# An adaLN block with a spectral filter and a SwiGLU on one core: load order, step order at the stage borders, and who does the x1 sums and the gate folds

## The chip, the core and the metric

The kernel runs on one core of one Trainium2 chip. Times are device microseconds of one execution; lower is better. The engines are named as in the profile: PE (TensorE matmul, PEld its weight loads), DVE (VectorE), ACT (ScalarE), POOL (GpSimd) and SP (SyncE, which here issues nearly all DMAs). "L302" is line 302 of the kernel before.

## The reference

Shapes: x is 2048 x 640 (S x D), all inputs bf16, F = 1728. Cut to what matters:

```python
mod = (silu(c) @ w_mod).reshape(1, 6, 1, 640)
sa, ca, ga, sb, cb, gb = mod[:, 0], mod[:, 1], mod[:, 2], mod[:, 3], mod[:, 4], mod[:, 5]
h = layernorm(x) * (1 + ca) + sa
X = rfft2(h) * (w_r + 1j * w_i)
x = x + ga * irfft2(X)
h = layernorm(x) * (1 + cb) + sb
x = x + gb * ((silu(h @ w_gate) * (h @ w_up)) @ w_down)
```

The Fourier transforms run over both axes (2048 and 640) and are computed as matmuls with tables.

## The kernel before

The 2048 rows lie on 128 partitions as 16 tiles t (row = 16 p + t). The order of all work is written out by hand: each engine runs its instructions in the order in which the program issues them, and the framework adds the semaphores. SP's queue runs its DMA issues in program order too, so an issue that waits holds all later ones.

**Phase 1, forward transform, tile by tile.** Steps with one or two letters are listed in a string `plan` (L391) and called one after the other. For tile t: `T` transposes x on PE (L258), `h` copies the result to `hT_all` (L261, ACT), `G` forms sums on PE (L266), `d` the statistics on DVE (L272, L274), `m` a small copy of the mean (L277, ACT), `p` and `r` root and reciprocal for a pair of tiles (L281 on ACT, L285 on DVE), `s` scales the row table by the tile's 1/sigma into `Gs` (L290, L291; POOL, for tiles 0 and 15 DVE), `B` the transform along D on PE (L296, PSUM `zps`, one buffer), `Z` takes the mean out (L302, DVE), `S` the first part of the transform along S on PE (L310, L311), `A` copies the result to `A_sb` (L321, ACT). `ca`, `ms`, `mh` and others compute the modulation vectors that phase 1 needs. `keep_warm` (L240) issues idle matmuls at the start.

**Loads.** SP issues x and the table G in groups of four tiles, then four DMAs (L196) that write the filter's rows in reversed order, 128 bytes a row, to a scratch tensor `Wneg` in DRAM, with two small ones each for the wrapped row; then `wm_sa`, `Ktab`, the filter itself (`Wb`, L205), the reversed filter (`Wq`, L207) and `KIt`.

**Phase 2, units of four columns.** 17 units u (unit 16 holds a single column). `t2` (L436) transposes a unit on PE, `transposed` (L432) two units by DMA. Then a software pipeline over `it`: `product(it)` multiplies by the filter on DVE (L487), `stage_x(it + 1)` computes the next unit's `xps` on PE and copies it to `X` on ACT (L466), where POOL adds a small term (L469); `stage_y(it - 1)` computes `yps` on PE and copies it to `Y2` (L509, ACT or DVE); `stage_e(it - 2)` computes `eps_` on PE and copies it to `Ep` (L539, ACT). All PSUM tiles of this phase rotate through four slots. `negate` (L412) prepares negated copies of the filter, for the first 33 columns on POOL (L416), and `mirror` (L548) those of `Ep` on DVE. Between iterations stand three groups of modulation matmuls: 50 at `it == 8` for the gate ga and for cb, the gate's transpose at `it == 9` (L229; its row goes to DRAM and comes back spread over the partitions by `gate_spread`, L238), 25 at `it == 10` for sb.

**Phase 3, inverse transform, tile by tile.** `s1inv` (L680) makes ten matmuls and a copy `VT` on ACT (L688); `dinv` (L692) five matmuls, then adds x to give x1: on DVE (L706), or, for the six tiles in `X1_ACT`, by five more matmuls (L702) and a copy on ACT (L704). The second layernorm's statistics of tiles 0 to 3 (`ln2_stats`, L626), their normalization (`ln2_xn`, L649, DVE), a DMA transpose (`ln2_turn`) and the affine step (`ln2_affine`, L660, DVE for even and ACT for odd blocks) are placed among the tiles.

**Feed-forward.** Four chunks sc of 512 rows. For each: `gu13` (L745), then 13 blocks fc of ten matmuls into `gu` (L757, two PSUM buffers), Silu on ACT (L760) and the product on DVE (L761). Into these blocks the next chunk's layernorm is placed: statistics at fc 1 to 4, `ln2_newton` (L632, twelve small DVE steps) at fc 5, `xn` at 6 and 7. In the first chunk the gate gb is folded into the rows of `Wd_sb` by DVE (L770), at the blocks that `folds` (L739) names. Then come the down matmuls (L795) and those of the last half block of 64 rows (`down13`, L790), and the sum with x1 and the store (L806, L809). For the last chunk's last half tile the accumulator is a fourth buffer of tag "o" (L786).

Of the kernel before, what the change touches and what calls it, by code (L numbers as in the profile page):

```python
# [104 lines left out]
def adaln_block_kernel(  # L105
# [83 lines left out]
    for g in range(1, 4):  # L189
        nc.sync.dma_start(x_sb[:, 4 * g:4 * g + 4, :], x_v[:, 4 * g:4 * g + 4, :])  # L190
        nc.sync.dma_start(Gtab[:, 4 * g:4 * g + 4], G_dram[:, 4 * g:4 * g + 4])
    for i, w_ in enumerate((A_w_i, A_w_r)):
        wv = w_.rearrange("(k2 k1) l -> k2 k1 l", k1=P)[:, :, 64:320]
        to = Wneg[i].rearrange("k1 k2 m l -> k2 k1 m l")
        for m in range(2):
            nc.sync.dma_start(to[:, 1:128, m], wv[:, 127:0:-1, 128 * m:128 * m + 64])  # L196
        w0 = wv[:, 0].rearrange("k2 (m l) -> k2 m l", m=2)[:, :, 0:64]
        nc.sync.dma_start(to[0:15, 0], w0[1:16])
        nc.sync.dma_start(to[15:16, 0], w0[0:1])
# [4 lines left out]
    for pl, w_ in ((0, A_w_i), (1, A_w_r)):  # L204
        nc.sync.dma_start(Wb[:, pl, :, 0:321], w_.rearrange("(k2 k1) l -> k1 k2 l", k1=P))  # L205
    for i in range(2):
# [37 lines left out]


    A_sb = big.tile([P, NL, NT, 2, NR], BF16, name="A_sb", tag="a")
    A_fl = A_sb[:].rearrange("p l t c r -> p (l t c r)")
    with tc.tile_pool(name="ph1", bufs=3) as ph1, \
# [64 lines left out]
        def acopy(t):  # L313
            ap = apss.pop(t)
            o = A_sb[:, :, t, :, :]
            i = ap[:, :, 0:325].rearrange("p c (r l) -> p l c r", r=NR)
            if t == NT - 1:
                nc.scalar.copy(o[:, 0:33], i[:, 0:33])
                nc.vector.tensor_copy(o[:, 33:NL], i[:, 33:NL])
            else:  # L320
                (nc.vector.tensor_copy if t in A_DVE else nc.scalar.copy)(o, i)  # L321
# [27 lines left out]
        def rv_out(_):  # L349
            nc.scalar.activation(rv, rvs[0][:].rearrange("p b q -> p (b q)")[:, 0:D], ACT.Copy, scale=0.2)  # L350
# [4 lines left out]
        keep_warm(ps1, "t1", 32)  # L355
# [28 lines left out]
        def sa_out(_):  # L384
# [4 lines left out]
        HT_DVE, A_DVE, S_DVE = (), (), (0, 15)  # L389
        GROUP = {0: 1, 1: 2, 3: 2, 5: 2, 7: 2, 9: 2, 11: 2, 13: 2, 15: 1}  # L390
        plan = (  # L391
# [6 lines left out]
        )  # L398
        steps = {"ca": mod_ca, "oc": one_ca, "rsD": rs_dve, "rsA": rs_act, "rvp": rv_mm, "rv": rv_out, "T": turn, "h": turned, "G": sums,
                 "d": stats, "m": mean, "p": root, "r": recip, "s": gscale, "B": dfwd, "Z": zcopy, "S": s1, "A": acopy,  # L400
                 "ms": mod_sa, "sacs": sa_cs, "mh": mod_sahat, "sh": sa_out}
        for w in plan.split():
            n = w.rstrip("0123456789")
            steps[n](int(w[len(n):] or 0))

# [5 lines left out]

    def negate(lo, hi, eng):  # L412
        eng(Wbr[:, 96:144, lo:hi], Wbr[:, 0:48, lo:hi])

    def neg_pool(o, i):
        nc.gpsimd.tensor_scalar(o, i, neg1[:], None, ALU.mult)  # L416

    def neg_dve(o, i):
        nc.vector.tensor_scalar(o, i, neg1[:], None, ALU.mult)

    with tc.tile_pool(name="ph2", bufs=2) as ph2, \
# [14 lines left out]
        def t2(u):  # L436
# [6 lines left out]
            (nc.vector.tensor_copy if u in (1, 3) else nc.scalar.copy)(o, ps[:, 0:n])  # L443
# [3 lines left out]
        def stage_x(u):  # L447
# [17 lines left out]
            X = ph2.tile([P, NI, 4], BF16, name="X", bufs=3)  # L465
# [49 lines left out]
        def stage_e(u):  # L515
# [26 lines left out]
            if u == 0:  # L542
                put(63, 0, 1)
                put(0, 1, 3)
            else:
                put(4 * u - 1, 0, 4)

        def mirror(lo, hi, eng):  # L548
            eng(Ep[:, :, 130 + lo:130 + hi, :], Ep[:, :, lo:hi, :])

        Y_ACT, E_DVE = (1, 3, 5, 7, 9, 11, 13, 15), ()

        negate(0, 17, neg_pool)
        negate(17, 33, neg_pool)
# [6 lines left out]
        t2(2)  # L561
        t2(3)
        for j, i in enumerate((2, 4)):
            nc.sync.dma_start(wm_g[:, :, D * j:D * (j + 1)], wm_v[:, :, D * i:D * (i + 1)])
        for it in range(NU + 2):
            if it < NU:
                product(it)
            if it + 1 < NU:
                stage_x(it + 1)
            if 0 <= it - 1 < NU:  # L570
                stage_y(it - 1)
            if it == 8:
# [303 lines left out]
```

## Time and profile before

| what | us |
|---|---|
| median of 3 runs (lowest, highest) | 284.56 (284.25, 288.49) |
| the profiled execution | 284.64 |
| its span, first to last instruction | 282.8 |
| PE busy, DVE, ACT, POOL | 263.9, 156.6, 113.9, 29.2 |
| mean granted PE clock | 0.994 of full |

The profile's page gives busy time by engine and by group of instructions, and the chain of work that ended last; the trace behind it can be asked for a timeline, for waits, and for a table of any stretches of time. A line of a timeline has the start, the duration, the engine, the line, the operation, what it writes and reads, how often, and in brackets how long the engine was idle before it and what released it. Several instructions in a row with one form are merged. Matmuls overlap, so a matmul's own duration (220 ns for 128 columns) is longer than the step from one to the next (56 ns).

### The profile page before, as it was taken

How to read it: one execution, taken by the hardware profiler on the slowest of the kernel's cores; microseconds unless marked ns; L12 is line 12 of the kernel's file. 1: busy time of each engine (PE TensorE's matmuls, PEld its weight loads, DVE VectorE, ACT ScalarE, POOL GpSimd, SP SyncE). 2: the span in 40 equal slices, each digit the busy share in tenths (PEclk: the TensorE clock that was granted, in tenths of full speed). 3: DMA queues.
4: the chain of work that ended last, by engine and by line, in shares of the span. 5: the costliest groups of instructions: out<-in, count | busy, mean ns of one | idle time of the engine just before them, and what ended most of it. 6: DMA issues, size and time to landing. Idle time of an engine off the chain costs nothing.

```text
span 282.8 us, 5295 instructions
## 1 busy us (share of the span) xinstructions
PE 263.9 (93%) x2162; PEld 168.4 (60%) x2162; DVE 156.6 (55%) x369; ACT 113.9 (40%) x211; POOL 29.2 (10%) x55
## 2 busy tenths in 40 slices
PE   6899976999788989999999999999999999999985
PEld 6777755999678834445664445664444664444653
DVE  0587857968678417877335863243872253422133
ACT  5688746978667763223012324004222203223000
POOL 1076854211000000000000000000000000000000
PEclk9799999999999999999999999999999999999999
DMA  7979999978931691040010031021004021000011
GB/s 237 360 147 210 346 291 304 255 208 271 360 140 22 86 324 35 0 94 0 26 69 10 12 67 26 3 70 32 9 18 77 0 72 32 9 2 1 0 49 46
DMA packets 44693, 30.55 MB, mean 108 GB/s; under 512 B 28795, under 2 KB 41596, under 8 KB 44540
## 3 DMA queue, kind: packets, MB, share of 16 engines
q1 hardware_dynamic: 44666, 30.21, 38.1%
q8 instruction: 17, 0.28, 0.4%
q14 instruction: 8, 0.07, 0.1%
q10 hardware_dynamic: 2, 0.00, 0.0%
HBM read 22.46 MB, written 3.67 MB: 92 GB/s over the span
## 4 chain that ended last, share of the span: by engine, by line
PE 81%; DVE 7%; ACT 6%; issue 3%; POOL 2%; DMA 0%; ACTq 0%; DVEq 0%; POOLq 0%
PE gu L757 38%; PE oa L795 19%; PE yps L501 2%; ACT early L261 2%; PE va L686 2%; PE oab L700 2%; PE t1ps L266 2%; PE oab L702 2%; POOL Wb L416 1%; PE gu L745 1%; DVE PP L487 1%; PE w_ps L243 1%; PE m_ps L217 1%; PE zps L296 1%; DVE Z L302 1%
## 5 line engine op out<-in xcount | busy, mean ns | idle before, releaser
L757 PE MATMUL gu<-h2T_all,Wg 128*128 128x512 bf16 x260 | 64.6, 379 | 0.4 <-DVE late L761 0.4
L757 PE MATMUL gu<-h2T_all,Wu 128*128 128x512 bf16 x260 | 64.6, 379 | 0.0
L760 ACT ACTIVATE sg<-gu 128x512 f32<-128x512 f32 x52 | 31.0, 597 | 78.9 <-PE gu L757 74.2
L757 PEld LDWEIGHTS <-Wg 128*128 128x128 bf16 x260 | 25.3, 98 | 31.3 <-issue 1.1
L757 PEld LDWEIGHTS <-Wu 128*128 128x128 bf16 x260 | 25.4, 98 | 30.7
L806 DVE TENSOR_TENSOR xo<-oa,late 128x320 bf16<-128x320 f32 x31 | 19.9, 694 | 35.1 <-PE oa L790 20.6
L761 DVE TENSOR_TENSOR ATb<-gu,sg 128x512 bf16<-128x512 f32 x26 | 17.9, 690 | 31.7 <-ACT sg L760 31.6
L761 DVE TENSOR_TENSOR late<-gu,sg 128x512 bf16<-128x512 f32 x26 | 17.8, 686 | 22.7 <-ACT sg L760 22.7
L795 PE MATMUL oa<-Wd_sb,late 128*128 128x320 bf16 x208 | 29.2, 299 | 0.4 <-DVE Wd_sb L770 0.3
L795 PE MATMUL oa<-Wd_sb,ATb 128*128 128x320 bf16 x195 | 27.2, 299 | 0.0
L795 PEld LDWEIGHTS <-late 128*128 128x128 bf16 x208 | 20.1, 98 | 9.4 <-issue 1.4
L795 PEld LDWEIGHTS <-ATb 128*128 128x128 bf16 x208 | 20.1, 98 | 8.6 <-issue 0.3
L748 ACT ACTIVATE sg<-gu 64x512 f32<-64x512 f32 x4 | 2.3, 586 | 42.6 <-PE gu L745 42.6
L290 POOL TENSOR_SCALAR Gs<-Gtab,rstd 128x256 bf16<-128x256 bf16 x14 | 12.9, 923 | 16.8 <-DVE rstd L285 14.4
L302 DVE SCALAR_TENSOR_TENSOR Z<-rtile,negm,zps 128x640 bf16<-128x640 f32 x16 | 14.0, 875 | 0.9 <-PE zps L296 0.8
L686 PE MATMUL va<-Htab,Ep 128*128 128x128 bf16 x160 | 11.5, 220 | 1.6 <-ACT Ep L539 1.6
L688 ACT CAST VT<-va 128x640 bf16<-128x640 f32 x16 | 11.0, 692 | 4.6 <-PE va L686 4.5
L466 ACT CAST X<-xps 128x640 bf16<-128x640 f32 x16 | 11.3, 706 | 3.5 <-PE xps L464 3.5
L700 PE MATMUL oab<-Rinv_sb,VT 128*128 128x128 bf16 x80 | 10.6, 225 | 2.3 <-DVE late L706 1.1
L706 DVE TENSOR_TENSOR late<-oab,x_sb 128x640 bf16<-128x640 f32 x10 | 8.6, 863 | 7.4 <-PE oab L700 7.4
L501 PE MATMUL yps<-identb,PP 128*128 128x128 bf16 x130 | 10.1, 220 | 2.1 <-DVE PP L487 2.0
L261 ACT COPY early<-t1ps 128x640 bf16<-128x640 bf16 x16 | 11.0, 695 | 2.3 <-PE t1ps L258 2.1
(276 smaller groups left out, 379.5 us busy)
## 6 DMA issues: line engine op xcount, KB each, us to landing
out_dram<-xo SPq DMA_DIRECT2D x16, 160.0 KB, 1.8
Wg<-in_B_w_gate_dram SPq DMA_DIRECT2D x1, 2080.0 KB, 9.8
Wu<-in_B_w_up_dram SPq DMA_DIRECT2D x1, 2080.0 KB, 11.5
Wd_sb<-in_B_w_down_dram SPq DMA_DIRECT2D x1, 2080.0 KB, 8.8
x_sb<-in_A_x_dram SPq DMA_DIRECT2D x3, 640.0 KB, 9.5
early<-in_w_mod_dram SPq DMA_DIRECT2D x2, 800.0 KB, 4.8
wm_g<-in_w_mod_dram SPq DMA_DIRECT2D x2, 800.0 KB
Wb<-in_A_w_i_dram SPq DMA_DIRECT2D x1, 1284.0 KB, 8.5
```

The lines of the kernel that those rows point to most:

```text
L261: (nc.vector.tensor_copy if t in HT_DVE else nc.scalar.copy)(hT_all[:, t % HB, :, 0:128], t1s[t][:, 0:320].bitcast(BF16).rearrange("p (r q ...
L290: e.tensor_scalar(Gss[t][:, 0:2], Gtab[:, t], rstd1[:, t:t + 1], None, ALU.mult)
L302: nc.vector.scalar_tensor_tensor(Zs[t][:].rearrange("p r q -> p (r q)"), rv, negm[:, t:t + 1], z[:].rearrange("p b q -> p (b q)")[:, 0:D], ...
L466: nc.scalar.copy(X[:].rearrange("p q (b j) -> p q b j", b=2), xps[:, :, 0:2 * NI].rearrange("p b (j q) -> p q b j", j=2))
L501: nc.tensor.matmul(yf[:, 128 * j:128 * j + 128], lhsT=PP[:, cp, 0:128] if u == 16 else PP[:, cp, 0:128, j], rhs=identb[:], start=(cp == 0) ...
L686: nc.tensor.matmul(o, lhsT=Ep[:, t, 65 - 65 * f:193 - 65 * f, r], rhs=Htab[:, t, f, :], start=(f == 0), stop=(f == 1))
L700: nc.tensor.matmul(o, lhsT=VT[:, r, :], rhs=Rinv_sb[:, r, :], start=True, stop=t not in X1_ACT)
L757: nc.tensor.matmul(o, lhsT=w_[:, c5, fc * 128:(fc + 1) * 128], rhs=h2T[:, :, c5, :], start=(c5 == 0), stop=(c5 == NC5 - 1))
L760: nc.scalar.activation(sg[:], gu[:, 0, :], ACT.Silu)
L761: nc.vector.tensor_tensor(AT[:, fc, :], gu[:, 1, :], sg[:], ALU.mult)
L795: nc.tensor.matmul(acc[2 * tl + h][:, 0:320], lhsT=AT[:, fc, tl * 128:(tl + 1) * 128], rhs=Wd_sb[:, fc, h * 320:(h + 1) * 320], start=(tl ...
L806: nc.vector.tensor_tensor(xos[tl][:, h * 320:(h + 1) * 320].rearrange("p (a r) -> p a r", r=NR), acc[2 * tl + h][:, 0:320].rearrange("p (a ...
```

## The change

1. **Loads.** The four reversed-row DMAs are sent among the groups of x and G; the filter's planes alternate with the reversed planes; the first half of `wm_g` (gate ga) is loaded on SP right after `KIt`, its second half (cb) and `Rinv_sb` ahead of phase 2's loop.
2. **Start.** 12 idle matmuls in place of 32; another order of the first steps; `h` of tile 0 on DVE; the copy of `rv` in two parts on ACT and DVE.
3. **Plan.** `m` stands behind `h` and `Z` for every tile; the last `A` is whole on ACT; the two POOL negations are issued right after the plan.
4. **Phase 2.** `stage_x` runs two units ahead, with four `X` buffers; unit 16 is worked on before 14 and 15. The gate's 25 matmuls stand ahead of the loop and its transpose and spread at `it == 1`, ahead of the DMA transposes on SP; the other 50 modulation matmuls follow the loop, and so do the loads of `wm_gb` and `Wg`. The last unit's `Ep` copy is split between ACT and DVE; its `Y2` copy is on DVE; the last mirror is split in two.
5. **Phase 3.** All x1 sums are on DVE; no L702 matmul and no L704 copy is left. The statistics of tile t follow tile t's sum, t < 4; the normalized rows of the first chunk are made on ACT (`activation` with scale and bias) at t = 4 to 7; the affine steps stand at t = 12, 13 and 14. For tile 0 the matmuls that need no mirrored column come first.
6. **Feed-forward.** Seven folds (rows 7 to 13) are issued on POOL at fc 2, seven stay on DVE, one each at fc 4 and 6 to 11. In the last chunk the last half tile's 64-row matmul comes after its other thirteen.

The diff, cut:

```diff
+    load(1)
+    load(1, False)
+    turn_rows(0, 0)
+    load(2)
+    turn_rows(0, 1)
+    load(2, False)
+    turn_rows(1, 0)
+    load(3)
+    turn_rows(1, 1)
+    load(3, False)
     nc.sync.dma_start(wm_sa, wm_v[:, :, 0:D])
     nc.sync.dma_start(Ktab[:], K_dram)
...
+    for i, w_ in enumerate((A_w_i, A_w_r)):
+        nc.sync.dma_start(Wb[:, i, :, 0:321], w_.rearrange("(k2 k1) l -> k1 k2 l", k1=P))
         nc.sync.dma_start(Wqp[:, 2 - i], Wneg[i].rearrange("k1 k2 m l -> k1 (k2 m l)"))
     nc.sync.dma_start(KIt[:], KI_dram)
+    nc.sync.dma_start(wm_g[:, :, 0:D], wm_v[:, :, 2 * D:3 * D])
...
-        keep_warm(ps1, "t1", 32)
+        keep_warm(ps1, "t1", 12)
...
+            "T0 T1 h0 h1 G0 G1 d0 ca m0 d1 p0 r0 m1 oc rsD T2 rsA T3 h2 s0 rvp h3 B0 rvD G2 rv G3 d2 Z0 m2 p1 T4 r1 h4 d3 B1 "
+            "s1 S0 Z1 m3 G4 A0 T5 d4 s2 B2 h5 S1 Z2 m4 p3 G5 A1 T6 r3 d5 B3 s3 h6 S2 Z3 m5 G6 A2 T7 s4 d6 B4 h7 S3 Z4 m6 p5 "
...
+            "s13 ms2 ms3 Z13 m15 ms4 p15 S12 sacs s14 B14 r15 A12 s15 mh Z14 S13 sh B15 A13 S14 Z15 A14 S15 A15 "
...
+        negate(0, 17, neg_pool)
+        negate(17, 33, neg_pool)
...
+        Y_ACT = (1, 3, 5, 7, 9, 11, 13)
+        order = list(range(14)) + [16, 14, 15]
...
         stage_x(0)
         t2(2)
+        stage_x(1)
         t2(3)
+        m_ps = mods("m_ps", (wm_g, 0))
+        nc.scalar.copy(g_col[0][:], m_ps[:, 0, 0:NC5])
+        nc.sync.dma_start(wm_g[:, :, D:2 * D], wm_v[:, :, 4 * D:5 * D])
+        nc.sync.dma_start(Rinv_sb[:], Rinv_dram)
         for it in range(NU + 2):
             if it < NU:
+                product(order[it])
+            if it + 2 < NU:
+                stage_x(order[it + 2])
             if 0 <= it - 1 < NU:
+                stage_y(order[it - 1])
+            if it == 1:
                 gate_turn(slot("gT_ps")[0:NC5, 0, 0:64].bitcast(BF16), 0)
                 gate_spread(0)
             if 0 <= it - 2 < NU:
+                stage_e(order[it - 2])
+            if it in (2, 4, 6):
+                transposed(it + 6)
...
+        m_ps = mods("m_ps", (wm_g, 1), (wm_sb, 0))
+        nc.scalar.copy(modcols[:, 1, :], m_ps[:, 0, 0:NC5])
+        nc.scalar.add(one_p_cb[:], m_ps[:, 0, 0:NC5], 1.0)
+        nc.scalar.copy(modcols[:, 0, :], m_ps[:, 1, 0:NC5])
+        wm_gb = big.tile([P, NC5, D], BF16, name="wm_gb", tag="wsb")
+        nc.sync.dma_start(wm_gb[:], wm_v[:, :, 5 * D:6 * D])
+        Wg = big.tile([P, NC5, FFM], BF16, name="Wg", tag="wg")
+        nc.sync.dma_start(Wg[:], B_w_gate[:, 0:FFM].rearrange("(dp c5) f -> dp c5 f", dp=P))
...
+        for r in range(NR):
+            nc.tensor.matmul(of[:, 128 * r:128 * r + 128], lhsT=VT[:, r, :], rhs=Rinv_sb[:, r, :], start=True, stop=True)
+        nc.vector.tensor_tensor(x1[:, t, :].rearrange("p (r a) -> p r a", r=NR), of.rearrange("p (r a) -> p r a", r=NR),
+                                x_sb[:, t, :].rearrange("p (a r) -> p r a", r=NR), ALU.add)
...
+        if t in (4, 5, 6, 7):
+            nc.scalar.activation(xn2s[0][:, t - 4, :], x1[:, t - 4, :], ACT.Identity, scale=rstd2[:, t - 4:t - 3], bias=nb2[:, t - 4:t - 3])
...
-    folds = {5: (0,), 6: (1,), 7: (2,), 8: (3, 4), 9: (5, 6), 10: (7, 8), 11: (9, 10), 12: (11, 12, 13)}
+    folds = {4: 0, 6: 1, 7: 2, 8: 3, 9: 4, 10: 5, 11: 6}
...
+                for f in range(7, NFC) if fc == 2 else ():
+                    nc.gpsimd.tensor_tensor(Wd_sb[:, f, :], Wd_sb[:, f, :], g_bc[1][:], ALU.mult)
+                if fc in folds:
+                    f = folds[fc]
                     nc.vector.tensor_tensor(Wd_sb[:, f, :], Wd_sb[:, f, :], g_bc[1][:], ALU.mult)
...
+        def early(tl, h):
+            return tl > 1 and not (sc == 3 and tl == 3 and h)
```

More of the change, by code (lines that the diff above doesn't have):

```diff
@@ L768, in adaln_block_kernel @@
                     gate_spread(1)
-                for f in folds.get(fc, ()):
+                for f in range(7, NFC) if fc == 2 else ():
+                    nc.gpsimd.tensor_tensor(Wd_sb[:, f, :], Wd_sb[:, f, :], g_bc[1][:], ALU.mult)
+                if fc in folds:
+                    f = folds[fc]
                     nc.vector.tensor_tensor(Wd_sb[:, f, :], Wd_sb[:, f, :], g_bc[1][:], ALU.mult)
@@ L790, in down13 @@
             nc.tensor.matmul(acc[2 * tl + h][:, 0:320], lhsT=AT[r, 13, tl * 128:(tl + 1) * 128],
-                             rhs=Wd_sb[r, 13, h * 320:(h + 1) * 320], start=(tl > 1), stop=(tl < 2))
+                             rhs=Wd_sb[r, 13, h * 320:(h + 1) * 320], start=early(tl, h), stop=not early(tl, h))
         def down(tl, h):
@@ L796, in down @@
                                  rhs=Wd_sb[:, fc, h * 320:(h + 1) * 320],
-                                 start=(tl < 2 and fc == 0), stop=(tl > 1 and fc == NFC - 2))
+                                 start=(fc == 0 and not early(tl, h)), stop=(fc == NFC - 2 and early(tl, h)))
         xos = {}
@@ L822, in adaln_block_kernel @@
                 down(tl, h)
+                if not early(tl, h):
+                    down13(tl, h)
                 if sc == 3 and tl == 3:
```

165 lines of the change are left out of this document (63 added, 102 removed), and 9 rows, old and new, of the table plan.

## The prediction

> **What bounds the kernel now.** I read the clock first (0.994, one core), then the chain of waits, which is 81% TensorE (PE), then a table of stages, then the timeline of each border. The table, whose columns are busy time and (instructions) of PE, weight loads, VectorE (DVE), ScalarE (ACT) and GpSimd (POOL), granted clock, DMA share and GB/s:
>
> ```profile
> 0.00:13.30 13.30, 9.78 (x112) 8.94 (x113) 4.03 (x25) 7.60 (x18) 0.83 (x7) 0.87 0.86 291
> 13.30:39.80 26.50, 24.12 (x314) 18.60 (x312) 20.64 (x66) 20.22 (x49) 18.49 (x30) 1.00 0.94 266
> 39.80:45.80 6.00, 3.29 (x39) 2.49 (x39) 3.26 (x7) 3.27 (x5) 5.45 (x5) 1.00 1.03 204
> 45.80:75.30 29.50, 29.21 (x417) 26.05 (x417) 24.45 (x47) 24.09 (x44) 4.44 (x14) 1.00 0.97 273
> 75.30:77.00 1.70, 0.07 (x1) 0.03 (x1) 0.82 (x2) 0.71 (x1) 0.00 (x0) 1.00 0.99 376
> 77.00:101.20 24.20, 21.07 (x301) 18.55 (x302) 14.84 (x30) 17.08 (x27) 0.00 (x0) 1.00 0.43 114
> 101.20:132.30 31.10, 30.35 (x144) 13.83 (x143) 21.79 (x56) 11.31 (x20) 0.00 (x0) 1.00 0.30 80
> 132.30:282.80 150.50, 145.99 (x841) 79.87 (x840) 66.80 (x140) 29.60 (x49) 0.00 (x0) 1.00 0.11 30
> ```
>
> The reader is to see that PE is the bound in the loop over units (45.8 to 75.3) and in the feed-forward part, so matmuls taken out there count in full. Phase 1 (to 39.8) is a balance of four resources with DMA at 0.94, and the two borders (39.8 and 75.3) hold PE's idle time. In phase 1 the ACT timeline shows what a tile costs (a copy `A_sb` each):
>
> ```profile
> 29.30 0.70 ACT L321 CAST A_sb<-aps 128x650 bf16<-128x650 f32 x1
> 30.87 0.70 ACT L321 CAST A_sb<-aps 128x650 bf16<-128x650 f32 x1
> 32.10 0.16 ACT L277 COPY negm<-t1ps 128x1 f32<-128x1 f32 x1 [0.52 <-DVE v L274]
> 32.18 0.69 ACT L261 COPY early<-t1ps 128x640 bf16<-128x640 bf16 x1
> 32.87 0.69 ACT L321 CAST A_sb<-aps 128x650 bf16<-128x650 f32 x1
> ```
>
> The step from 29.30 is 1.57, the next 2.00: where the small copy `m` stands ahead of `h`, ACT waits.
>
> **The parts.** The sum is made against the profiled execution: span 282.8, its time 284.64 (1.84 around the span), 0.08 from the median 284.56.
>
> *Start.* 20 idle matmuls of 3.60/32 = 0.11 leave: 2.25. The first x tiles land at 0.72 + 3.0 = 3.7, where the first transposes now start at 5.6, so at most 1.9 is gained. What is late next: `wm_ca` (1.16 + 4.8 = 6.0) and the half clock that the table by single microseconds shows from 9.9 to 13.3 (0.50), which may stay where it is. I take -1.3, ends -1.9 and +1.5 (one more such stretch: a tile's 1.42 of PE doubles to 2.84, so 3.4 us lose 1.6).
>
> *Order of the tiles.* The plan puts `m` behind `h` and `Z` everywhere. The four steps with `m` first took 1.99, 1.84, 1.82 and 2.00, the others 1.52 on average: -1.6. The last copy whole on ACT is 0.69 in place of 38.85 to 39.81: -0.25. `h0` on DVE (about 0.49 by L443) lies beside `h1`. Phase 1 would end at 39.8 - 3.15 = 36.7.
>
> *DMA order.* That end is not what decides next. Between 15 and 25 us the four reversed transfers leave the DMA engines idle for about 3.5 us (shares of 0.64, 0.16, 0.62, 0.16, 0.70, 0.47, 0.75). Between x and G the gaps have other transfers to fill them. I take half, 1.9 (ends 0 and 3.5). The late pieces stay hidden: x tiles 12 to 15 would land near 21.5, wanted near 23; if that margin goes, each us late is a us lost. On SP's queue `KIt`, which drains at 39.9, then ends at 38.0; the gate's weights (0.82 MB) now follow it: 0.82 MB at 349 GB/s is 2.35, plus 1.5 from the last byte to the landing (as `KIt`), so 41.9. The 25 gate matmuls stand in PE's order ahead of units 2 and 3, so PE waits for them: 41.9 + 0.98 + 2 x 0.55 = 44.0 for the first `yps`, now 45.78: -1.8, and unit 3's `xps` (0.55) is done with it. Ends: -3.6 and +0.2.
>
> *First product.* The negations (L416) leave the queue behind the POOL memset that waited for phase 1's end; POOL is free from 35.9 - 3, so its 4.5 us end near 38 and X's sum no longer waits for 44.27. Covered by the wait above. If they meet `Gs` of tile 15 on DVE, up to 2.4.
>
> *Units.* 75 modulation matmuls leave the PE-bound stretch: 1.96 + 0.96 = 2.9, -2.9. X two units ahead buys nothing more there: PE idles 0.29 of 29.5. New: SP's queue holds the DMA transposes of units 8 and 9 behind the gate row and its spread, which waits until the row has landed (1.2 at L238, 2.3 for the second gate); I get a landing at 50 to 51 for an `xps` wanted at 50.5: +0.3 (0 to 2.5). The last unit's `Y2` copy on DVE, 0.82 plus 0.2, has only 0.54 of `eps_` beside it: +0.4. Last `eps_`: 75.3 - 1.8 - 0.55 - 2.9 - 0.05 + 0.7 = 70.7. Then 50 matmuls (1.96) in place of the 1.7 of waiting, with the last copies and mirrors under them: inverse starts at 72.5 to 72.7, now 77.0. **-4.4.**
>
> *Inverse.* 30 L702 matmuls go (six tiles of 1.56 become 0.84: 4.3 of PE), six x1 sums come to DVE (0.86 to 0.90 each). DVE becomes the bound: first sum 2.14 after the start, four tiles at 1.80 (sum and statistics, as 82.79 to 84.59), so tile 4's ends at 10.1. Then ACT has the four `xn2c` (0.61 back to back) between the `VT` copies, so sums 6 to 9 follow at 1.22, start + 1.24 behind each `VT`; sums to tile 14, a wait of 0.5 at the gate's matmuls, three DVE affines at 0.35, and 0.3 for the transposes: the first `gu` at 23.6, now 24.2. **-0.6** (all on DVE without ACT's part, -2.8; a second such wait, +1.5). `Wg` (9.8 to landing) and `wm_gb` issued at the border land 10 us before use.
>
> *Feed-forward.* These three gaps go: Newton no longer shares its step with a fold, no fold stands last, and the last half's matmuls wait for no early sum.
>
> ```profile
> 119.16 0.59 PE L757 MATMUL gu<-h2T_all,Wg 128*128 128x512 bf16 x2 [0.35 <-DVE late L761]
> 131.93 2.33 PE L795 MATMUL oa<-Wd_sb,late 128*128 128x320 bf16 x14 [0.32 <-DVE Wd_sb L770]
> 271.82 0.31 PE L790 MATMUL ob<-Wd_sb,ATb 64*128 64x320 bf16 x1 [0.98 <-DVE xo L806]
> ```
>
> **-1.65.** Up to here 284.64 - 4.4 - 0.6 - 1.65 = 278.0.
>
> *Folds on GpSimd.* Seven 128x640 folds, back to back on POOL from 110.0 (the spread gate lands at 106.56 + 3.0; times on the old clock). Do they disturb DVE? Rows of both engines:
>
> ```profile
> 34.61 0.92 POOL L290 TENSOR_SCALAR Gs<-Gtab,rstd 128x256 bf16<-128x256 bf16 x1
> 34.94 0.29 DVE L290 TENSOR_SCALAR Gs<-Gtab,rstd 128x256 bf16<-128x256 bf16 x1
> 47.69 0.53 DVE L487 TENSOR_TENSOR PP<-X,Wb 128x768 bf16<-128x768 bf16 x1
> 47.93 0.41 POOL L469 TENSOR_TENSOR X<-X,sahat 1x40 bf16<-1x40 bf16 x1 [2.66 <-ACT X L466]
> 48.15 0.66 DVE L487 TENSOR_TENSOR PP<-X,Wq 128x512 bf16<-128x512 bf16 x1
> 53.66 0.25 POOL L469 TENSOR_TENSOR X<-X,sahat 1x40 bf16<-1x40 bf16 x1 [1.70 <-ACT X L466]
> 54.93 0.54 DVE L419 TENSOR_SCALAR Ep<-Ep,neg 128x1200 bf16<-128x1200 bf16 x1
> 55.00 0.58 POOL L469 TENSOR_TENSOR X<-X,sahat 1x40 bf16<-1x40 bf16 x1 [1.09 <-ACT X L466]
> ```
>
> POOL's sum takes 0.25 alone, but 0.58 beside DVE's negation and ends 0.11 after it; DVE's next product takes 0.66 in place of 0.55 behind POOL's. So where both read two SBUF operands they take turns, one whole instruction each. Newton (L636 to L645, twelve DVE steps of 0.2) comes at 116, in the middle of the folds, and each of its steps would wait for one fold; `gu`'s product is queued behind it on DVE, and PE's second next `gu` behind that. A fold's price is not in the trace: 128 elements took 0.37 (1.25 for 640 with 0.15 fixed), 816 took 2.38 (1.86). I take the middle, 1.6: folds 7 to 9 end at 114.8, DVE's own fold waits for that, fold 10 ends at 117.0, then 11, 12 and 13 alternate with Newton's steps to 122.3; nine more steps and the product, 124.8; `gu` 8 was due at 118.5. **+6.3** (1.25: 3.5; 1.86: 8.1). So long a gap may halve the clock as at 9.9 (at most 1.65): +0.8. Sum: 278.0 + 6.3 + 0.8 = **285.1**.
>
> The first two rows speak against the turns: DVE's 0.29 is no longer than its other such step (0.28), inside POOL's 0.92. [...]
>
> **The rivals.** (1) The folds cost nothing, as steps of four elements do not wait or alternate: for it, the 34.94 row; against it, the 48.15 row. 278.0, chance 0.25. (2) Slower: each fold takes 2.4 or more, for two inputs (the 256 element row has 3.6 ns an element, 2.3 for 640). At 2.4 `gu` 8 comes 11.9 late: 278.0 + 11.9 + 0.8 = 290.7. It ends above the old time from about 1.6 on, over 2% above from 2.4. Chance 0.12. (3) The loads gain nothing: gate weights at 43.9 (+2.0) and the transposes of unit 8 late in full (+2.2): 285.1 + 4.2 = 289.3; for it, DMA at 0.94 to 1.03; against it, the idle shares. Chance 0.13.
>
> **The numbers.** Forecast 0.46, rivals 0.25, 0.12, 0.13, the rest 0.04. About 2% (5.7) is what a measurement of this kernel can tell from no change. Faster (below 278.9): two thirds of rival 1 (0.17), the forecast's low tail (0.05) and 0.02 = 0.24. Slower (above 290.3): rival 2 (0.12) and tails of rival 3 and the rest (0.03) = 0.15. Within: 0.61. The likeliest alone: 281.5 to 288.5. The range leaves out a third of rival 1 and most of rival 2: 277 to 290.
>
> **What would show it.** Right: `A_sb` copies 1.5 apart throughout; the first gate matmul waiting on `wm_g`; inverse start near 72.6; no PE gaps at the three rows above; Newton stretched from 2.2 to 6 or more between GpSimd folds, with one PE gap of 3 to 8 at a `gu`. Wrong: a Newton of 2.2 beside running folds (rival 1); folds of 2.4 (rival 2); `yps` at 45.8 or later, or `xps` of unit 8 waiting for a DMA (rival 3).

## The result, and the profile after

The changed kernel takes 296.27 us (median; 294.22 to 297.94), the kernel before 284.40 beside it: a ratio of 1.042, 95% interval 1.033 to 1.050. It is slower by about 12 us, where the forecast was 285.1 and the range ended at 290. The profiled execution took 296.92, its span is 295.1, its granted clock 0.960.

The table by stage of the changed kernel, with the columns of the one shown before (borders: last `A_sb` copy, first gate matmul, 0.2 behind the first `yps`, first `va`, 0.6 behind the first `gu` on Wg, 141.0, which is 3.1 ahead of the first down matmul, end):

```profile
0.00:39.50 39.50, 32.94 (x403) 24.85 (x404) 25.32 (x91) 27.10 (x65) 18.46 (x35) 0.96 0.88 236
39.50:49.77 10.27, 2.55 (x32) 2.05 (x32) 2.12 (x3) 3.27 (x5) 5.33 (x3) 0.85 1.13 266
49.77:53.09 3.32, 3.32 (x39) 2.86 (x40) 2.06 (x4) 0.86 (x2) 0.73 (x3) 0.50 0.89 179
53.09:82.76 29.67, 28.06 (x387) 24.87 (x385) 25.61 (x50) 23.75 (x43) 6.47 (x14) 0.99 0.81 220
82.76:109.80 27.04, 21.61 (x273) 19.35 (x273) 18.91 (x33) 17.46 (x27) 0.00 (x0) 0.81 0.53 159
109.80:141.00 31.20, 26.50 (x116) 11.47 (x114) 21.68 (x45) 7.49 (x14) 9.75 (x7) 0.95 0.32 85
141.00:295.10 154.10, 150.63 (x869) 82.37 (x866) 68.97 (x144) 32.20 (x53) 0.00 (x0) 1.00 0.10 29
```

The reader is to see three places: PE busy 2.55 of 10.27 us at the first border, and a granted clock of 0.50 behind it, 0.81 in the inverse and 0.95 in the first chunk. By milestones (first `yps`, first `va`, first `gu` on Wg, end) the kernel before has 45.8, 77.0, 101.1, 282.8 and the changed one 52.9, 82.8, 109.2, 295.1. The differences stage by stage are +7.1, -1.3, +2.3 and +4.2, 12.3 in all; the forecast had -1.8, -2.6, -0.6 and +5.5.

The first border on SP, POOL and PE (timeline of the changed kernel, whose line numbers are its own):

```profile
26.97 6.16 SPq L219 DMA_DIRECT2D Wq<-Wneg  x1
...
33.74 7.08 SPq L219 DMA_DIRECT2D Wq<-Wneg  x1
40.86 0.43 SPq L220 DMA_DIRECT2D KIt<-tab_KI  x1
41.34 0.43 SPq L221 DMA_DIRECT2D wm_g<-in_w_mod_dram  x1
41.87 1.54 SPq L408 DMA_DIRECT2D sahat<-sh  x2
...
39.59 5.03 POOL L263 TENSOR_SCALAR Wb<-Wb,neg 128x816 bf16<-128x816 bf16 x2 [5.91 <-DMA Wb<-in_A_w_i_dram]
...
50.30 0.47 POOL L483 TENSOR_TENSOR X<-X,sahat 1x40 bf16<-1x40 bf16 x2 [5.39 <-DMA sahat<-sh]
...
49.77 1.16 PE L230 MATMUL m_ps<-sc_col,wm_g 128*128 128x1 bf16 x25 [6.51 <-DMA wm_g<-in_w_mod_dram]
50.79 0.43 PE L473 MATMUL xps<-Ktab,B2all 128*128 128x320 bf16 x1
...
52.88 0.91 PE L515 MATMUL yps<-identb,PP 128*128 128x128 bf16 x8
```

The same queue before:

```profile
34.41 0.44 SPq L208 DMA_DIRECT2D KIt<-tab_KI  x1
...
37.06 1.52 SPq L387 DMA_DIRECT2D sahat<-sh  x2
```

An issue on SP can take 0.4 us (`KIt`). Those that last 6 or 7 us wait for no semaphore that the profile names, so I read them as held back by what was issued ahead of them. `KIt` leaves 6.4 us later, and two consumers wait: PE for the gate's weights (6.51), POOL's first sum on X for `sahat`, two rows of 1.3 KB each (5.39). The negations of `Wb`, which the change issues early, waited 5.91 for `Wb` itself.

The inverse on DVE, ACT and PE (timeline), with the table by two microseconds:

```profile
93.01 0.30 ACT L238 ACTIVATE rstd<-mv,eps_t 128x4 f32<-128x4 f32 x1 [2.60 <-DVE mv L645]
...
94.01 0.92 ACT L729 ACTIVATE xn2c<-late,nb,rstd 128x640 bf16<-128x640 bf16 x1 [0.70 <-DVE nb L726]
94.83 0.67 ACT L704 CAST VT<-va 128x640 bf16<-128x640 f32 x1
...
95.56 0.72 PE L712 MATMUL oab<-Rinv_sb,VT 128*128 128x128 bf16 x5 [2.70 <-ACT VT L704]
```

```profile
84.00:86.00 2.00, 1.64 (x17) 1.61 (x17) 0.79 (x1) 0.93 (x2) 0.00 (x0) 0.56 0.86 298
...
96.00:98.00 2.00, 2.00 (x22) 2.00 (x21) 0.96 (x2) 2.00 (x4) 0.00 (x0) 0.50 0.24 52
```

ACT waits for the fourth tile's statistics, and the copy `VT` that PE needs is queued behind that wait: PE idles 2.70, and its clock is at half from 94.5 to 101.3. A first stretch at half lies from 84.2 to 87.6.

The folds (timeline; DVE's Newton steps, POOL's folds, PE's gap):

```profile
119.60 9.75 POOL L777 TENSOR_TENSOR Wd_sb<-Wd_sb,gb_bc 128x640 bf16<-128x640 bf16 x7 [42.77 <-DMA gb_bc<-gb_row]
...
124.21 1.12 DVE L651 TENSOR_SCALAR veps<-mv 128x4 f32<-128x4 f32 x1
125.36 1.32 DVE L653 TENSOR_SCALAR rs_yi<-veps 128x4 int32<-128x4 int32 x1
126.72 1.31 DVE L654 TENSOR_SCALAR rs_yi<-rs_yi 128x4 int32<-128x4 int32 x1
128.06 1.31 DVE L658 TENSOR_TENSOR rs_t<-rs_yi 128x4 f32<-128x4 f32 x1
129.41 0.16 DVE L659 SCALAR_TENSOR_TENSOR rs_t<-rs_t,veps 128x4 f32<-128x4 f32 x1
...
131.60 1.93 PE L764 MATMUL gu<-h2T_all,Wg 128*128 128x512 bf16 x5 [4.70 <-DVE late L768]
```

Four of the twelve small steps take 1.1 to 1.3 us, one fold each, until POOL's last fold ends at 129.35; then a step takes 0.16 again.

### The profile page after: what moved, and what is told of

Its sections match the earlier page's. It is cut to its first block, busy times and chain, and to the rows that moved or that the text cites. A ratio compares the mean times of both kernels' runs of the same rounds, so it can differ in the third digit from the quotient of the medians.

```text
span 295.1 us, 5212 instructions
## 1 busy us (share of the span) xinstructions
PE 265.6 (90%) x2112; PEld 167.8 (57%) x2112; DVE 164.7 (56%) x369; ACT 112.1 (38%) x207; POOL 40.7 (14%) x62
## 4 chain that ended last, share of the span: by engine, by line
PE 66%; SPq 13%; DVE 10%; DMA 5%; issue 2%; ACT 2%; ACTq 0%; DVEq 0%
PE gu L764 35%; PE oa L808 19%; SPq L219 4%; SPq L192 4%; DMA wm_g<-in_w_mod_dram 3%; DMA B2all<-A_sb 3%; SPq L200 2%; PE va L701 2%; PE gu L752 1%; PE oab L712 1%; DVE late L713 1%; DVE PP L501 1%; PE yps L515 1%; DVE st L643 1%; PE m_ps L230 1%
## 5 line engine op out<-in xcount | busy, mean ns | idle before, releaser
L764 PE MATMUL gu<-h2T_all,Wg 128*128 128x512 bf16 x260 | 65.3, 382 | 4.7 <-DVE late L768 4.7
L764 PE MATMUL gu<-h2T_all,Wu 128*128 128x512 bf16 x260 | 65.6, 384 | 0.0
L713 DVE TENSOR_TENSOR late<-oab,x_sb 128x640 bf16<-128x640 f32 x16 | 13.8, 862 | 8.3 <-PE oab L712 7.9
L755 ACT ACTIVATE sg<-gu 64x512 f32<-64x512 f32 x4 | 2.4, 590 | 42.0 <-PE gu L752 41.9
L777 POOL TENSOR_TENSOR Wd_sb<-Wd_sb,gb_bc 128x640 bf16<-128x640 bf16 x7 | 9.8, 1428 | 42.8 <-DMA gb_bc<-gb_row 42.8
L312 POOL TENSOR_SCALAR Gs<-Gtab,rstd 128x256 bf16<-128x256 bf16 x14 | 12.9, 922 | 14.6 <-DVE rstd L307 10.6
L701 PE MATMUL va<-Htab,Ep 128*128 128x128 bf16 x160 | 14.4, 251 | 0.4 <-ACT modcols L628 0.4
L712 PE MATMUL oab<-Rinv_sb,VT 128*128 128x128 bf16 x80 | 8.9, 255 | 5.4 <-ACT VT L704 4.2
L704 ACT CAST VT<-va 128x640 bf16<-128x640 f32 x16 | 10.9, 688 | 5.7 <-PE va L701 5.5
L701 PEld LDWEIGHTS <-Ep 128*128 128x128 bf16 x160 | 12.6, 129 | 0.4 <-issue 0.4
L501 DVE TENSOR_TENSOR PP<-X,Wb 128x768 bf16<-128x768 bf16 x16 | 9.0, 562 | 6.8 <-POOL X L483 6.8
```

What stands on the lines that cost most here:

```text
L312: e.tensor_scalar(Gss[t][:, 0:2], Gtab[:, t], rstd1[:, t:t + 1], None, ALU.mult)
L501: nc.vector.tensor_tensor(bass.AP(o.tensor, o.offset, [o.ap[0], [4 * NI, 2], [2 * NI, 2], [4, n], [1, 4]]), bass.AP(xi.tensor, xi.offset, ...
L701: nc.tensor.matmul(vf[:, 128 * r:128 * r + 128], lhsT=Ep[:, t, 65 - 65 * g:193 - 65 * g, r], rhs=Htab[:, t, g, :], start=(f == 1 and r in ...
L712: nc.tensor.matmul(of[:, 128 * r:128 * r + 128], lhsT=VT[:, r, :], rhs=Rinv_sb[:, r, :], start=True, stop=True)
L713: nc.vector.tensor_tensor(x1[:, t, :].rearrange("p (r a) -> p r a", r=NR), of.rearrange("p (r a) -> p r a", r=NR), x_sb[:, t, :].rearrange ...
L764: nc.tensor.matmul(o, lhsT=w_[:, c5, fc * 128:(fc + 1) * 128], rhs=h2T[:, :, c5, :], start=(c5 == 0), stop=(c5 == NC5 - 1))
```

## The experiments

Two theories of the lost 12 us stood against each other at the start: that the new order of the loads makes the first border late and the folds the rest, or that PE's clock, which falls after each gap, does. Ratios are to the kernel before, run beside each. The medians of the kernel before in these comparisons run from 284.40 to 286.44, so a median of one experiment less that of another is good to some 2 us only. Kernels with the same loads scatter at the first border by as much in their profiles: e11 and e17, below, have one code up to there and their first `yps` at 44.6 and 47.0. So ratios carry the verdicts and profiles the mechanism.

**The order of the loads, undone in full and by halves.** e1 undoes both edits below, e2 only the second, e3 only the first.

```diff
-    load(1)
-    load(1, False)
-    turn_rows(0, 0)
-    load(2)
...
+    for g in range(1, 4):
+        load(g)
+        load(g, False)
+    for i in range(2):
+        turn_rows(i, 0)
+        turn_rows(i, 1)
...
     for i, w_ in enumerate((A_w_i, A_w_r)):
         nc.sync.dma_start(Wb[:, i, :, 0:321], ...)
+    for i in range(2):
         nc.sync.dma_start(Wqp[:, 2 - i], ...)
```

> The changed kernel with the load order of before (x and G in full, then the reversed rows, then both planes of Wb and both of Wq); the first gate weights stay behind KIt, all else stays changed. Theory L (the new order of the loads holds SP back: KIt is issued at 40.86 in the changed kernel, at 34.41 before, and the gate's weights come that much later): KIt issued near 34.4, gate weights landed near 43.5, first yps near 46, time 296.3 - 7 = about 289.5. Rival R (the border is late because PE itself waits for the gate's weights and its clock is halved there, or because what is gained there is lost again to the transposes of units 8 to 14): less than 3 us come back, 293.5 or more. If the forecast's term for the loads had been right in size, 296.3 would stay.

> The changed kernel with one part of the load order undone: Wb, Wb, Wq, Wq in place of Wb, Wq, Wb, Wq; the reversed rows stay among x and G. From the issue of the first Wb to that of KIt the changed kernel takes 14.4 us, the one before 9.0. If the alternation of the planes makes this 5.4: KIt issued near 35.5, time about 291. If the reversed rows make it (their small pieces still being in the queue when the planes are issued): time stays at 295 to 296.5.

> The changed kernel with the other part of the load order undone: the reversed rows behind all of x and G, the planes still alternating. The weights behind them (wm_sa) are issued at 25.46 in the changed kernel, at 23.54 before. If the rows cost only that: time about 294.4. If the rows carry all of the 6.4 us: about 289.5. If the alternation carries what is left, the sum of this gain and that of the run with the planes undone is the gain of the run with both undone.

Measured: 292.78, 295.29 and 292.40 us, ratios 1.022 (1.015 to 1.029), 1.032 (1.026 to 1.038) and 1.023 (1.016 to 1.030). Undoing the rows brings back some 1.9%, the planes 1.0%, both together no more than the rows alone. `KIt` was issued at 37.6, 38.7 and 36.7, not at 34.4, and PE still waited 7.4, 7.5 and 4.7 us for the gate's weights. For the full undoing that is 3.5 us by the medians and 5.6 by the ratios, of the 7 expected; the first `yps` came at 50.6, not at 46. The order is one cause among others.

**All folds on DVE, outside Newton's step** (e4).

```diff
-                for f in range(7, NFC) if fc == 2 else ():
-                    nc.gpsimd.tensor_tensor(Wd_sb[:, f, :], Wd_sb[:, f, :], g_bc[1][:], ALU.mult)
-    folds = {4: 0, 6: 1, 7: 2, 8: 3, 9: 4, 10: 5, 11: 6}
+    folds = {4: (0,), 6: (1,), 7: (2,), 8: (3, 4, 5), 9: (6, 7, 8), 10: (9, 10), 11: (11, 12, 13)}
```

> The changed kernel with all 14 folds on DVE, none in the step that holds Newton's steps and none in the last; GpSimd folds nothing. Theory F (Newton's steps take turns with GpSimd's folds): the gap of 4.7 us at the second gu behind Newton goes, and the half clock behind it (2.6 us at half speed, 1.3 lost), Newton takes 2.2, time 296.3 - 6 = about 290.3. Rival (DVE itself is full there, and with seven more folds it stops PE anyway): a gap of 2 or more stays in this stage, time 293 or more.

Measured: 289.92, ratio 1.014 (1.007 to 1.020), 2.8% below the changed kernel's ratio (8.0 us; 6.4 by the medians). Newton's steps in its timeline:

```profile
124.62 0.16 DVE L651 TENSOR_SCALAR veps<-mv 128x4 f32<-128x4 f32 x1
124.82 0.17 DVE L653 TENSOR_SCALAR rs_yi<-veps 128x4 int32<-128x4 int32 x1
...
126.88 0.68 DVE L768 TENSOR_TENSOR late<-gu,sg 128x512 bf16<-128x512 f32 x1
```

2.2 us, and no gap of PE: from first `gu` to the end 179.4 against 185.9. Theory F holds.

**The kernel before, a second time; the inverse as before; the gate's matmuls in the loop; and a mix** (b0, e5, e6, e8). e5 puts back the loop over tiles with `X1_ACT`. e6 is e1 with this edit, e8 is e6 with the edits of e4 and e5:

```diff
-        m_ps = mods("m_ps", (wm_g, 0))
-        nc.scalar.copy(g_col[0][:], m_ps[:, 0, 0:NC5])
...
+            if it == 8:
+                m_ps = mods("m_ps", (wm_g, 0))
+                nc.scalar.copy(g_col[0][:], m_ps[:, 0, 0:NC5])
-            if it == 1:
+            if it == 9:
                 gate_turn(slot("gT_ps")[0:NC5, 0, 0:64].bitcast(BF16), 0)
```

> The kernel before, unchanged, profiled a second time. In its first profile the planes of Wb move at 343 to 349 GB/s (30 to 36 us); in the profiles of the changed kernel and of the run with the old load order they move at 272 to 281, with the DMA engines just as full (shares of 1.12 and 1.13). If that rate differs from execution to execution: 275 to 350 here, first yps up to 2 us later than 45.8, and ratio 1.00. If the changed kernel lowers it (a denser phase 1, or another place of the data): 349 here again and yps at 45.8.

> The changed kernel with the loop over tiles of the inverse as before: six sums through TensorE and ScalarE, the rest on DVE, statistics at tiles 2 to 5, Newton and the normalised rows on DVE at tile 7. In the changed kernel first va to first gu on Wg takes 26.4 us, with 2.7 us of waiting for VT behind xn2c on ACT and the clock at half from 95 to 101; before it took 24.1. Theory I (DVE's 1.9 us a tile in the first four tiles, then ACT's chain, let PE fall idle and halve its clock): 24 us again, time 296.3 - 2.3 = 294. Rival (the part is as long as before, and what is lost in it is a cold clock brought along from the border): 296 or more.

> The run with the old load order, and besides the 25 gate matmuls moved from ahead of unit 2 into the loop over units at it 8 (their turn and spread at it 9); their weights are still issued behind KIt. With the old load order alone PE waits 7.4 us for these weights, and the first yps comes at 50.6. Theory G (the wait on the gate's weights sets the border): the wait is gone, the first yps comes when the first product is ready, at 44 to 46, and 1.0 us of matmuls goes back into the stretch that PE bounds: time 292.8 - 4 = about 289, with no half clock behind the border. Rival (the product itself is as late, since it waits for the planes of Wb and Wq and their negation): yps at 49 to 50, time 292 or more.

> The run with the old load order and the gate matmuls in the loop, and besides the inverse as before and all folds on DVE: what is left of the change is the plan of phase 1, fewer idle matmuls, X two units ahead, the modulations at the second border, the split of the last unit's copies, and the feed-forward part without its three gaps. If the terms add up: 289 - 2.3 - 6 = about 281, faster than both kernels. If the gains of phase 1 are lost to the loads whatever their order: 284 to 285.

Measured: b0 285.73, ratio 1.002 (0.998 to 1.006), planes again at 349 GB/s, first `yps` again at 45.8. e5 293.23, 1.030 (1.026 to 1.033); but its inverse took 26.3, as in the changed kernel, and what it gained lies ahead of the first `yps` (50.9): not what theory I said; e18 below gives a cause for it. e6 295.01, 1.036 (1.033 to 1.039): no gain, first `yps` at 49.2, PE now waiting 3.7 for the first product. Theory G fell. e8 285.21, 1.001 (0.999 to 1.004): what is left of the change is worth nothing in the sum.

**What holds the first product?** In e8 it is POOL's sum, which waits for `sahat`. e9 issues the gate's weights behind the first transposes; e10 issues `sahat` from ACT's queue; e12 does both; e11 is the kernel before with e10's edit.

```diff
-    nc.sync.dma_start(wm_g[:, :, 0:D], wm_v[:, :, 2 * D:3 * D])
...
-                nc.sync.dma_start(sahat[0:1, cc, :, 0:NL], sh5[:, cc, :])
+                nc.scalar.dma_start(sahat[0:1, cc, :, 0:NL], sh5[:, cc, :])
...
         t2(3)
+        nc.sync.dma_start(wm_g[:, :, 0:D], wm_v[:, :, 2 * D:3 * D])
```

> The mixed run, with the first half of the gate's weights issued behind the first units' transposes, as in the kernel before, in place of right behind KIt. In the mixed run the two rows of sahat (1.3 KB) are issued at 35.0 and 35.8 and GpSimd's first sum on X waits for them until 44.6; the first yps comes at 46.1. Theory Q (the rows stand in SP's queue behind every load issued ahead of them, 0.82 MB of gate weights among them, at the 400 GB/s of that stretch 2.0 us): first sum near 42.5, first yps near 44, time 285.2 - 2 = about 283. Rival (Wb, Wq and their negations are not ready sooner, and the rows only land with them): first yps stays at 45.5 to 46, time 285.

> The mixed run, with the two rows of sahat issued from ScalarE's queue in place of SP's; the gate's weights stay right behind KIt. Theory Q: the rows no longer stand behind the loads and land 2 to 3 us after their issue, near 38; the first product then waits for the negated planes alone, first yps at 41 to 43, time 285.2 - 4 = about 281. Rival (the 16 DMA engines are full, shares of 1.0 and more, so rows from another queue come no sooner): first sum near 44.5 again, time 285.

> The kernel before with that one edit: the rows of sahat issued from ScalarE's queue. There GpSimd is at its own negations until the first sum at 44.3 (2.0 busy in each 2 us from 40 to 44). Theory (two bounds at the same time there, rows and negations): no change, 284.5 to 285.5. Rival (the rows alone set the border before as well): 281 to 282.

> The mixed run with both edits: gate weights behind the first transposes, and the rows of sahat on ScalarE's queue. If the rows were all that the gate's weights held up: as the run with ScalarE's queue alone, about 281. If the weights also hold up the DMA transposes of units 4 and 6 or KIt: 1 to 2 us less, 279 to 280. If the loads of Wb and Wq bound the border behind the rows: 283.

POOL's first sum in e8, e9 and e10:

```profile
44.60 1.58 POOL L480 TENSOR_TENSOR X<-X,sahat 1x40 bf16<-1x40 bf16 x4 [5.81 <-DMA sahat<-sh]
```

```profile
42.44 1.58 POOL L479 TENSOR_TENSOR X<-X,sahat 1x40 bf16<-1x40 bf16 x4 [3.41 <-DMA sahat<-sh]
```

```profile
41.61 0.44 POOL L480 TENSOR_TENSOR X<-X,sahat 1x40 bf16<-1x40 bf16 x1 [1.71 <-ACT X L477]
```

Theory Q holds for the place: without the weights ahead of them the rows come 2.2 us sooner, and from ACT's queue they are no longer what POOL waits for. The first `yps` moves from 46.1 to 44.0, 44.4 and (e12) 44.3, not to the 41 to 43 that were expected of e10: in e10 and e12 DVE's negation waits 1.7 and 1.9 for `Wq`. The times follow in part: 283.95, 284.19 and 284.02, ratios 0.996 (0.993 to 0.999), 0.994 (0.990 to 0.998) and 0.997 (0.993 to 1.001), so 0.4 to 0.7% (1.2 to 2.1 us) below e8, where 2 to 6 us were expected; e11 284.77, 0.998 (0.994 to 1.001). One place where time is lost again stands in the chain of waits of e12:

```profile
45.45 8.53 DMA B2all<-A_sb
...
61.71 3.45 DMA ga_row<-gTa
65.18 3.07 DMA ga_bc<-ga_row
```

The next units' DMA transposes land 8.5 us after their issue and PE waits 1.9 for them (1.2 in e9, 2.2 in e10, no such wait in e8); then DVE waits for the gate's row. From the first `yps` to the first `va` e12 takes 34.1, e8 31.4. The execution of e8 that was profiled was its fastest (282.93), so its 31.4 may be short for it; but the waits show that the loop loses to its own DMAs a part of what the border gains.

**The gate's weights alone, and the load order alone** (e13: the changed kernel with the gate's matmuls in the loop and their weights behind; e16: the kernel before with the changed loads up to `KIt`; both by edits shown above).

> The changed kernel with two edits: the first half of the gate's weights is issued behind the first transposes (as before), and its 25 matmuls stand in the loop over units at it 8. The reversed rows stay among x and G, the planes alternate, the folds stay on GpSimd. If the gate's weights ahead of the rows of sahat, and PE's wait for them, make most of the border's 7.3 us: first yps at 46 to 47, time 296.3 - 6 = about 290. If the order of rows and planes makes it (KIt is issued 6.4 us later than before): first yps at 49 to 50, time about 293, or ratio near 1.03.

> The kernel before with one edit: the changed order of the loads as far as KIt (reversed rows among x and G, planes alternating); the gate's weights stay behind the first transposes. If this order alone holds the queue back: KIt issued at 38 to 41 in place of 34.4, first yps at 48 to 50, time 285 + 3 = about 288. If the order only costs where the gate's weights follow it: first yps near 46, time 285. As the prediction had it (1.9 us of idle DMA time filled): first yps near 44, time 283.

Measured: e13 295.59, 1.035 (1.029 to 1.040), first `yps` at 48.5 in place of 52.9, half of the 4.4 lost again by the first `gu` (107.0 in place of 109.2). e16 287.26, 1.006 (1.002 to 1.010), `KIt` at 39.5, first `yps` at 47.2. So the order alone costs the kernel before 0.6% (1.8 us); that its first `yps` came 1.4 later is within the scatter of the profiles.

**Idle matmuls in the gaps** (e14).

```diff
+        idle(slot("w_ps"), 100)
         m_ps = mods("m_ps", (wm_g, 0))
...
         m_ps = mods("m_ps", (wm_g, 1), (wm_sb, 0))
+        idle(slot("w_ps"), 8)
...
             s1inv(t + 1)
+        if t == 6:
+            idle(o2("w_ps"), 30)
```

> The changed kernel with idle matmuls of 128 columns in three gaps of PE: 100 ahead of the gate's matmuls at the first border, 8 behind the 50 modulation matmuls at the second, 30 in the inverse between the va of tile 7 and the oab of tile 6. Every wait stays. Theory C (each gap is followed by 3.3 to 3.7 us of matmuls at half clock, and this is what the later stages lose): no half clock at 50 to 53, 84 to 87 and 95 to 101, so 1.9 + 1.6 + 3 us less, 290 to 292; the inverse takes 24 instead of 26.4. Rival (the stages are bound by DVE, ACT and DMA there, and PE's clock only changes how it waits): 295 to 297.

Measured: 296.25, 1.037 (1.030 to 1.044). The clock is full up to the folds (0.988 over all), and still nothing that the interval could tell is gained; the inverse takes 25.1. Theory C falls as the main cause: at these places PE mostly waits, at whatever clock.

**The version that the runs point to** (e17): the kernel before with the changed feed-forward part, e4's folds, and `sahat` on ACT's queue.

> The kernel before with the changed feed-forward part, all 14 folds on DVE outside Newton's step and none in the last, the matmuls of the 14th slice of the last half behind the others, and the rows of sahat on ScalarE's queue. The prediction's term is 1.65 for the three gaps; ScalarE's queue gave 0.7 alone. If both hold: 285.2 - 2.4 = about 282.8, ratio 0.99. If the gaps only move: 284.5, ratio 0.998.

Measured: 282.78 against 285.33, ratio 0.990 (0.986 to 0.994): 1% faster than the kernel before, clear of 1 by the interval, though under the 2% that the prediction took as the least to be told. The execution that was profiled was its slowest (285.99), so only its last stage is read: 179.5 from first `gu` to the end, 181.7 before.

**The place of the data.** One thing was left: with the changed inverse, `Wb` loads at 270 to 281 GB/s in every profile wherever it moves alone, with the old one at about 349. The changed inverse declares one more tile of constants, `nb2`, and `Wb` begins 32 bytes later in each partition.

```diff
-    nb2 = const.tile([P, 4], F32, name="nb2")
+    nb2 = ph4.tile([P, 4], F32, name="nb2", bufs=1)
```

```diff
     Wp13 = const.tile([P, NC5, 128], BF16, name="Wp13")
+    pad = const.tile([P, 4], F32, name="pad")
```

> The changed kernel with one edit: the tile nb2 (16 bytes a partition) is taken from a pool behind the big tiles, so that Wb begins at byte 119648 of each partition, as in the kernel before, in place of 119680. No instruction changes. Theory A (where Wb begins sets the rate at which its 642 byte rows land): Wb at 349 GB/s in place of 275, 2.57 MB are 2.0 us faster, gate weights and first yps 2 us earlier, time 296.3 - 2 = about 294.3. Rival (the rate goes with something else in these kernels): 275 GB/s, 296.

> The kernel before with one edit: a tile of 16 bytes a partition that nothing reads is declared among the constants (and set to zero once), so that the big tiles lie 32 bytes later and Wb begins at byte 119680. Theory A: Wb at 275 GB/s in place of 349, first yps 1 to 2 us after 45.8, time 285.2 + 1.5 = about 286.7. Rival: 349 GB/s, first yps at 45.8, time 285.

Measured: e18 293.10, ratio 1.025 (1.021 to 1.030), 1.7% below the changed kernel's (4.7 us; 3.2 by the medians), first `yps` at 49.5 in place of 52.9; e19 288.52, 1.006 (1.001 to 1.010). One microsecond of this stretch in the kernel before, in e19, in the changed kernel and in e18 (columns as in the table by stage):

```profile
34.00:35.00 1.00, 1.00 (x22) 0.94 (x21) 0.91 (x3) 0.82 (x3) 1.00 (x3) 1.00 1.12 349
```

```profile
34.00:35.00 1.00, 0.71 (x15) 0.68 (x15) 0.54 (x3) 0.96 (x3) 0.23 (x1) 1.00 1.14 277
```

```profile
39.00:40.00 1.00, 0.46 (x4) 0.19 (x2) 0.00 (x0) 0.55 (x2) 0.41 (x1) 1.00 1.12 278
```

```profile
38.00:39.00 1.00, 0.51 (x10) 0.51 (x9) 0.00 (x0) 0.44 (x1) 1.00 (x2) 1.00 1.12 349
```

Theory A holds both ways for the rate. No instruction differs between e18 and the changed kernel but in its addresses. All big tiles move by the 32 bytes, not `Wb` alone, so the rate is read on the rows of `Wb`, while the time may hold other parts.

## Why the prediction was wrong, point by point

**DMA order: the step that failed** (-1.8 forecast, +7.1 measured). The path was as forecast: PE waits for the gate's weights, then makes 25 matmuls and two units' `xps` ahead of the first `yps`. The term that failed is the landing of these weights, 41.9 forecast and 49.7 measured; `KIt`, which was to end at 38.0, was only issued at 40.86. The matmuls behind it took 3.1 in place of 2.1. The runs show four causes.

First, "I take half, 1.9" of the idle DMA time as filled: none was. From 15 to 28 us, one minus the share summed over single microseconds is 3.6 us on average in the profiles with the changed rows, and 3.5 in those with the old order (2.5 to 4.8 in single profiles). As I read it, the transfers of 128 byte rows stay what the queue waits for (in the kernel before the DMA engines move 25 to 202 GB/s in single microseconds from 16 to 25 us), and x and G now wait among them. The alternation then holds `KIt` back: issued at 38.4 to 41.3 with the changed order, at 34.0 to 37.6 with the old one. Second, "X's sum no longer waits for 44.27" counted one releaser where there were two. POOL's negations filled POOL up to that time in the kernel before, and I read them as the wait; but `sahat` stood in SP's queue, and the change put 0.82 MB of gate weights ahead of it (e9: 2.2 us). The negations themselves, forecast to end near 38, ended at 44.6, since they waited for `Wb`. Third, no term of mine had the place of `Wb`: 2.63 MB at 277 instead of 349 GB/s are 9.5 instead of 7.5 us, 2.0. Fourth, the two units' `xps` from 50.79 to the first `yps` ran at half clock, 2.1 in place of 1.1 (the 25 one-column matmuls took 1.0 at either clock).

These sizes (order 1.4 from e16, weights 2.2, place 2.0, clock 1.0) add up to 6.6 of the 7.1, but each comes from another pair of kernels, within the scatter named above. Undone one at a time in the changed kernel, the same four bring the first `yps` forward by 2.3 (e1), 4.4 (e13), 3.4 (e18) and 2.8 (e14, where `KIt` also left 1.9 sooner), 12.9 in all. So they overlap, and how the 7.1 is shared among them stays open. What is shown is the whole: with the order and the place of before and the gate's matmuls in the loop, the first `yps` is back at 46.1 (e8), and with the gate's weights behind as well at 44.0 (e9).

**Start and plan** (-3.15 forecast for the end of phase 1). The last matmul into `aps` starts at 37.3 on average in the profiles with the new plan, at 38.7 in those with the old: -1.4. The tiles themselves went as forecast: up to 30.15 the `A_sb` copies of the changed kernel come 1.4 to 1.6 apart, but for one step of 1.98. The earlier end gained nothing that the times show (e8), and I take it that the loads set what follows; the changed kernel itself lost 2.02 us to `wm_sa`, also late.

**Units** (-2.6 forecast from first `yps` to first `va`, -1.3 measured). The 75 matmuls did leave: the last `eps_` ended 27.4 after the first `yps`, forecast 26.7. The border behind it took 2.5, forecast 1.9: the copies after the 50 matmuls are waited for (0.39).

**Inverse** (-0.6 forecast, +2.3 measured). "DVE becomes the bound" was right; a tile cost 1.9, not 1.80. What I missed is that `VT` of tile 6 queues on ACT behind the statistics' chain, and the half clock. Without half clock at its start the changed inverse takes 25.1 (e13, e14), the old one 24.1 (before, b0, e8, e11, e12, e16): 1.0 is the code, 1.3 the clock in the changed kernel. The same half clock hits the old code too: 25.6 to 26.3 in e5, e9 and e10. What starts it there is open: it came in ten of thirteen profiles with 50 one-column matmuls ahead of it, but also in two of six without. Left open too, since not tried: folds on POOL that keep clear of Newton's steps, and other places for `Wb`.

**Feed-forward gaps** (-1.65 forecast). 179.4 to 179.5 in e4 and e17 against 181.7: -2.2. Right, a little undersized.

**Folds** (+6.3 and +0.8 forecast). 185.9 against 179.4: +6.5 with the clock. The mechanism was right in place and kind: a gap of 4.70, half clock for 3.4 us behind it. A fold took 1.43 on average, not 1.6; of the two ends, the lower (1.25) has 0.15 as fixed, my estimate, where POOL's shortest steps before took 0.10 (a memset of one element) and 0.20 (a sum of six). The turns stand in the trace: the four stretched DVE steps, of four elements each, took 1.12 to 1.32 beside folds (L658 1.31) and ended 0.02 to 0.03 after the end of a fold; behind the last fold L658 took 0.16. The prediction's "where both read two SBUF operands" is too narrow, since the three stretched steps ahead of L658 are TENSOR_SCALAR, with one tensor each. Nor does every DVE step take turns: beside the same folds the statistics kept their 0.47 to 0.48 and the product of `gu` its 0.64 to 0.69. What decides it no run here shows.

**Rivals.** The third (loads gain nothing, 289.3) had the right place, and its "yps at 45.8 or later" came true; but it put the border 2.0 above the forecast, where 8.9 came. I bounded the loads at +2.0 because I let them only fail to gain; that an order can lose was not in the range. The total of 296 is the forecast's folds plus a border that none of the four cases had.

## What to carry to other kernels

Ask of each small transfer which big ones stand ahead of it on its queue, and of each border what is second in line: here behind `sahat` stood `Wq`, and behind that the transposes of the next units, and a border 2 us sooner brought 1 to 2 us where 2 to 6 were expected. A load put "into idle DMA time" has to be costed as able to lose. When a change adds a tile, compare the addresses of the big tiles before its timing is explained by its code: e5 looked like a gain of the old inverse, lay ahead of the inverse, and by e18 is for the most part 32 bytes.

## What the runs showed of the hardware

- Rows of 642 bytes into SBUF, 768 bytes apart, move at 349 GB/s when the tile starts at byte 119648 of a partition and at 270 to 281 at 119680, with the DMA engines equally full (1.12 to 1.14): a factor of 1.27 (349 to 275). The runs have these two places alone; what it is in the place that makes the rate they do not show.
- PE's half clock came after a single wait of 2.02 us (30.1 to 32.1): from 33.0 to 36.4 in the changed kernel.

```profile
32.13 0.36 PE L387 MATMUL mpsB<-sc_col,early 128*128 128x1 bf16 x5 [2.02 <-DMA early<-in_w_mod_dram]
```

```profile
33.00:34.00 1.00, 1.00 (x21) 0.89 (x19) 0.95 (x4) 0.26 (x2) 0.68 (x2) 0.51 1.13 275
```

  In the traces' records of the granted clock, without the last stretch at half of an execution, those of the changed kernel last 3.41 us (three) and 6.83 (two), the one of the kernel before 3.41. How long a wait has to be for one no run here shows.
- On SP the issue of the first plane of `Wb` lasted 0.43 us in the kernel before, that of the second, in the same form and right behind it, 4.24; two issues in the changed kernel lasted 6.2 and 7.1. I read the queue itself as a wait there.
